# The last matmul stage of an attention and two-MoE kernel: operands of its Strassen products on VectorE alone, and a third output chunk ahead of the first product group

## The chip, the cores and the metric

The kernel runs on one core of one Trainium2 chip. The metric is device microseconds of one launch, from the first to the last instruction and what lies around it. Three runs of the kernel before took 625.68, 630.52 and 633.74 us; the median is 630.52.

## What is computed

Three parts run one behind the other. Attention with 12 heads mixes its scores over the heads before and after the softmax; its output, 896 tokens (two batches of 448) by 768, goes through two feed-forward layers:

```
x = attention(q, k, v, w_pre, w_post)       # (896, 768)
h = x @ w_in;   g = elu(h);   x = g @ w_out   # w_in (768, 2048), w_out (2048, 768)
h = x @ w2_in;  g = h * sigmoid(h);  out = g @ w2_out
```

The change lies in the last product, `g @ w2_out`. Everything is float32; each matmul operand is split in two parts, hi (the value rounded to the type that TensorE takes, fp32r) and lo (value minus hi), and a product is the sum hi*hi + hi*lo + lo*hi.

## The kernel before, in words

Output is held transposed: 6 row chunks c0 to c5 of 128 model columns, each by 896 tokens, that is by two halves of 448 tokens (each a matmul of 448 columns into one PSUM bank). The contraction over 2048 hidden units is 16 blocks f0 to f15 of 128. For f0 to f9 a chunk is computed classically, in two parts of five blocks (`moe_out`, line 527 and below): 5 blocks x 3 terms x 2 halves = 30 matmuls. The last six blocks f10 to f15 are done for two chunks at once by Strassen's scheme in Winograd's form: a 2x2 block product with seven products instead of eight. Each product (`prod2`, line 1050) is three blocks x three terms = 9 matmuls; seven make a pair of 63 matmuls. The left operands come from the weights, the right ones (B11, B21, B22, T1, T2, T3, T4) from the activations: B11 and T3's source are the first and second token half of f10 to f12, B21 and B22 those of f13 to f15; T1 = second half of f10 to f12 minus B11, T2 = B22 - T1, T3 = second half of f10 to f12 minus B22, T4 = B21 - T2. Each of the seven is split into hi (a cast on ScalarE) and lo (a subtraction on VectorE), for three blocks. They are made once, and all three pairs use them.

The program is written out by hand: each engine runs its instructions in the order of the code, and nothing is reordered. Engines are tied by semaphores. Around every chunk of weights stands the same row of work: a load of raw 64-bit words on SyncE's queue into one of two buffers (`load_w`, L435), a rescaling on ScalarE (`scale`, L755), two bit operations on VectorE (`bits0` and `bits1`, L746 and L751), a cast to hi on ScalarE (`split_hi`, L489), a subtraction to lo on VectorE (`split_lo`, L498). The result goes to one of four weight buffers (`wbuf`, tile `we`). A classical chunk takes one of the four, a Strassen pair all four (`hi_of` L735, `lo_of` L547, and sums of two weight chunks in `sums12`, `sum3`, `sum4`, L547 and L759). A chunk is loaded two chunks ahead, when the bit operations have emptied the raw buffer.

The order of the output stage (loop over j) is: classical parts of two chunks (120 matmuls), then their Strassen pair, three times. The first classical part of c0 lies already inside the end of the stage ahead, whose last products (lines 803 and 812 to 816) make f14 and f15; three classical parts (90 matmuls) then stand before the first pair. In these three parts `g_sums` (line 1024) makes the seven operands: one block at a time, 448 columns an instruction. The four subtractions T1 to T4 of each block, and the lo part of B22, go to GpSimd (POOL, L1030); the other lo parts go to VectorE (L547), the hi parts to ScalarE (L1034). In the pair, product B11 goes into a PSUM bank that ScalarE copies out (`one`, L1115) before product T2 adds to that bank.

Of the kernel before, what the change touches and what calls it, by code (L numbers as in the profile page):

```python
# [17 lines left out]
P = 128  # L18
# [17 lines left out]
KS = 10  # L36
KB = -(-S // BI)
# [38 lines left out]
def attn_moe_moe(ctx: ExitStack, tc: tile.TileContext, q, k, v, w_pre, w_post, w1i, w1o, w2i, w2o, out):  # L76
# [323 lines left out]
    for w in (w1i, w1o, w2i, w2o):  # L400
# [37 lines left out]
    def ring(n):  # L438
        return (O2 + (n - O2) % 6 if n >= O2 else n) % (NE + 1)
# [566 lines left out]
    x = [t[:, i] for t in rt for i in range(3)] + rk[:3]  # L1006
    for f in range(KF):
        raw[1, f] = x[f % 12]
    hb[1] = rk[3:]
    x = [ge[u][:, i] for u in range(2) for i in range(3)] + [gs[:, i] for i in range(6)]  # L1010
    x += [xt[1][a, i] for a in ("B11", "B21", "T2", "T1", "T3", "T4", "B22") for i in range(3)]
    for f in range(KS):
        gop[1, f] = x[2 * f:2 * f + 2]
    xs = x[2 * KS:]
    ob = [raw[1, f] for f in (4, 5)]
# [8 lines left out]
    def g_sums(i):  # L1024
        r1, r2 = raw[1, KS + i], raw[1, KS + 3 + i]
        t1, t2, t4 = (mo["eg"][:, j] for j in range(3))
        src = {"B11": r1[:, 0], "B21": r2[:, 0], "B22": r2[:, 1], "T1": t1, "T2": t2, "T3": r1[:, 1], "T4": t4}

        def psub(o, x, y):
            nc.gpsimd.tensor_tensor(o, x, y, op=ALU.subtract)  # L1030

        def sp(a):
            t = xt[2][a, i]
            nc.scalar.copy(t[:, 0], src[a])  # L1034
            (psub if a == "B22" else sub)(t[:, 1], src[a], t[:, 0])
# [12 lines left out]
    xs += [rg[:, i] for i in range(3)] + [None]  # L1048
    xt[2] = {(a, i): xs.pop(0) for a in ("T1", "T3", "B11", "B21", "T2", "B22", "T4") for i in range(3)}

    def prod2(o, d, u, x, start=False):
        hi, lo = wbuf[d]
        n_ = 0
        for wt, xi in ((hi, 0), (hi, 1), (lo, 0)):
            for i in range(3):
                nc.tensor.matmul(o, wt[:, u * KH + i * P:u * KH + (i + 1) * P], xt[2][x, i][:, xi], start=start and n_ == 0, stop=n_ == 8, skip_group_check=True)  # L1056
# [10 lines left out]
    def o_dma(c, hf, x=slice(0, S), eng=None):  # L1067
        (eng or nc.sync).dma_start(out[c * P:(c + 1) * P, hf * S + x.start:hf * S + x.stop], ob[hf][:, c % 2, x])

    def o_add(c, hf, a, parts=1):  # L1070
        for i in range(parts):
            x = slice(i * S // parts, (i + 1) * S // parts)
            nc.vector.tensor_tensor(ob[hf][:, c % 2, x], state[1, c][hf][:, x], a[:, x], op=ALU.add)
            o_dma(c, hf, x, (nc.sync, nc.scalar)[i])

    for j in range(3):
        n0, c0 = O2 + 6 * j, 2 * j
        a, b_ = n0 + 4, n0 + 5
# [122 lines left out]
```

## Time and profile before

| | |
|---|---|
| median of three runs | 630.52 us |
| profiled execution | 625.0 us, its span 623.2 us |
| mean granted TensorE clock | 0.989 of full |
| TensorE busy | 596.3 us, 96% of the span |
| VectorE busy | 457.7 us, 73% |
| ScalarE busy | 373.1 us, 60% |
| GpSimd busy | 84.9 us, 14% |

A busy TensorE is a modelled figure. The granted clock is the share of full speed that TensorE was given in a stretch: 1.0 is 2.4 GHz, 0.5 is 1.2 GHz. In the profile, PE is the matmuls, PEld the weight loads that overlap them, DVE is VectorE, ACT ScalarE, POOL GpSimd, SP SyncE; L1056 is line 1056 of the kernel before. Names of tiles stand without their numbers: `we` the weight buffers, `wr` raw weights, `wc` weights after the bit operations, `po` an output bank, `q` a Strassen bank, `rt` and `rk` activations, `eg` scratch.

### The profile page before, as it was taken

The numbers are of one execution on the slowest core, as the hardware profiler recorded it, in microseconds if no ns is written. First come the engines' busy times: TensorE is split into PE (matmuls) and PEld (weight loads), VectorE is DVE, ScalarE is ACT, GpSimd is POOL, SyncE is SP. The second block draws the span as 40 slices with busy tenths as digits, with TensorE's granted clock in tenths as the row PEclk, the third lists the DMA queues.
The fourth block names the chain that finished last, engine by engine and source line by source line (L and its number), as shares of the span: only waits on it lengthen the run. The fifth ranks groups of instructions, "written<-read, shape, count | busy, mean of one in ns | idle before, by whom it ended". The sixth has DMA issues, their size and how long they took to land.

```text
span 623.2 us, 15033 instructions
## 1 busy us (share of the span) xinstructions
PE 596.3 (96%) x6139; PEld 509.2 (82%) x6139; DVE 457.7 (73%) x761; ACT 373.1 (60%) x698; POOL 84.9 (14%) x132
## 2 busy tenths in 40 slices
PE   7899999998999999999999999999999997699997
PEld 3456666565799899999999999999999995599996
DVE  4776776787747998967775755798888889854552
ACT  4676776778748867578755533577766663532321
POOL 1222222257440000000000000000000326000000
PEclk9999999999999999999999999999999997799999
DMA  6587558745313343422334344243342231352701
GB/s 235 197 231 218 161 136 215 215 147 201 129 53 103 101 127 127 136 85 88 119 115 136 94 143 119 84 154 123 131 140 97 86 102 42 110 191 86 218 14 59
DMA packets 37682, 82.04 MB, mean 132 GB/s; under 512 B 4205, under 2 KB 18285, under 8 KB 37613
## 3 DMA queue, kind: packets, MB, share of 16 engines
q1 hardware_dynamic: 36749, 80.08, 41.0%
q8 instruction: 48, 0.79, 0.5%
q10 hardware_dynamic: 864, 1.00, 0.5%
q14 instruction: 21, 0.17, 0.1%
HBM read 59.05 MB, written 2.75 MB: 99 GB/s over the span
## 4 chain that ended last, share of the span: by engine, by line
PE 74%; DVE 11%; ACT 7%; DMA 4%; issue 2%; ACTq 0%; POOL 0%; DVEq 0%; SPq 0%; POOLq 0%
PE po L541 26%; PE b L803 25%; PE av L262 4%; ACT pe L209 4%; PE q L1056 3%; DMA blk<-s 3%; PE post L234 3%; PE pre L195 3%; PE ph L527 3%; PE pq L147 3%; PE po L1056 2%; DVE nmx L201 2%; DVE a L133 1%; PE post L527 1%; DVE rr L547 1%
## 5 line engine op out<-in xcount | busy, mean ns | idle before, releaser
L803 PE MATMUL b<-x,we 128*128 128x448 f32 x360 | 93.7, 363 | 0.0
L209 ACT ACTIVATE pe<-pre,nmx 124x448 f32<-124x448 f32 x90 | 56.3, 630 | 37.4 <-DVE nmx L201 36.5
L755 ACT ACTIVATE wr<-wr 128x768 f32<-128x768 f32 (+1 forms) x61 | 52.7, 864 | 36.7 <-DMA wr<-in_w2o_dram 21.9
L803 PEld LDWEIGHTS b<-x,we 128*128 128x128 f32 x360 | 67.5, 188 | 4.6
L803 PE MATMUL b<-rr,we 128*128 128x448 f32 x288 | 69.5, 362 | 0.0
L234 PEld LDWEIGHTS post<-krn,pe 60*64 60x64 f32 x2520 | 46.0, 135 | 22.7 <-issue 11.1
L541 PE MATMUL po<-gs,we 128*128 128x448 f32 x216 | 60.3, 362 | 0.0
L541 PE MATMUL po<-ge,we 128*128 128x448 f32 x216 | 60.3, 362 | 0.0
L751 DVE SCALAR_TENSOR_TENSOR wc<-wr,wc 128x768 int32<-128x768 int32 (+1 forms) x62 | 57.0, 920 | 2.7
L498 DVE TENSOR_TENSOR we<-wc,we 128x640 fp32r<-128x640 f32 (+1 forms) x31 | 27.7, 894 | 40.2 <-ACT we L489 40.1
L803 PEld LDWEIGHTS b<-rr,we 128*128 128x128 f32 x288 | 54.1, 188 | 3.5
L201 DVE TENSOR_REDUCE nmx<-pre 124x1 f32<-124x448 f32 x90 | 51.6, 614 | 5.2 <-PE pre L195 4.7
L541 PE MATMUL po<-x,we 128*128 128x448 f32 x204 | 54.4, 362 | 0.0
L222 POOL TENSOR_SCALAR krn<-kps,sum 124x60 f32<-124x60 f32 x90 | 37.8, 435 | 114.2 <-DVE sum L218 97.4
L234 PE MATMUL post<-krn,pe 60*64 60x60 f32 x2520 | 47.3, 219 | 4.1 <-POOL krn L222 2.8
L262 PEld LDWEIGHTS av<-a,v 128*64 128x64 f32 x768 | 36.9, 137 | 17.4 <-ACT pe L209 6.3
L195 PE MATMUL pre<-blk,kpre 64*64 64x448 f32 x360 | 47.4, 543 | 2.4 <-DMA blk<-s 1.7
L541 PE MATMUL po<-ta,we 128*128 128x448 f32 x168 | 44.8, 362 | 0.0
L147 PE MATMUL pq<-kt,qt 64*64 64x448 f32 x336 | 41.8, 564 | 2.8 <-ACT s L154 2.2
L1030 POOL TENSOR_TENSOR eg<-rk 128x448 f32<-128x448 f32 x2 | 2.9, 1436 | 300.9 <-ACT rk L816 300.9
L262 PE MATMUL av<-a,v 128*64 128x120 f32 (+1 forms) x768 | 41.8, 262 | 2.0 <-ACT a L131 2.0
L541 PEld LDWEIGHTS po<-ge,we 128*128 128x128 f32 x216 | 40.6, 188 | 2.6
(166 smaller groups left out, 1165.0 us busy)
## 6 DMA issues: line engine op xcount, KB each, us to landing
blk<-s SPq DMA_DIRECT2D x77, 210.0 KB
wr<-in_w1i_dram SPq DMA_DIRECT2D x32, 384.0 KB
wr<-in_w2i_dram SPq DMA_DIRECT2D x32, 384.0 KB
wr<-in_w1o_dram SPq DMA_DIRECT2D x24, 384.0 KB
wr<-in_w2o_dram SPq DMA_DIRECT2D x24, 384.0 KB
wr<-in_w1o_dram SPq DMA_DIRECT2D x12, 256.0 KB
wr<-in_w2o_dram SPq DMA_DIRECT2D x12, 256.0 KB
v<-in_v_dram SPq DMA_DIRECT2D x14, 192.0 KB
```

Source lines behind the costliest of these rows:

```text
L147: nc.tensor.matmul(pq[e][HS * c:HS * c + HS], qT[T][half, p, HS * c:HS * c + HS], kT[p][half, bs[c % len(bs)]], start=True, stop=True, til ...
L195: nc.tensor.matmul(pre[s][r][HS * c:HS * c + HS], kpre[o], blkb[o, s % NBUF, c], start=True, stop=True, tile_position=(HS * r, HS * c))
L201: nc.vector.tensor_reduce(nmx[s][:n, r:r + 1], pre[s][r][:n], axis=AX.X, op=ALU.max, negate=True)
L209: nc.scalar.activation(t[:n], pre[s][r][:n], AF.Exp, bias=nmx[s][:n, r:r + 1], scale=1.0, accum_out=sums[s][:n, r:r + 1])
L222: nc.gpsimd.tensor_scalar(t[:n], kps[:n], z[:n, r:r + 1], None, op0=ALU.mult)
L234: nc.tensor.matmul(w[c][HS * u:HS * u + HS, r, j * BW:(j + 1) * BW], pexp[s][r][o, m * HS:(m + 1) * HS], kr[s][r][o].rearrange("p h i -> p ...
L262: nc.tensor.matmul(avt[T][e * D:(e + 1) * D, p % 2, :m], vall[b][:NV, h, j], amap[T][:NV, j * H + h, :m], start=j == 0, stop=j == 3, tile_ ...
L541: nc.tensor.matmul(po, wt[:, kk * P:(kk + 1) * P], g_op(moe, k0 + kk, hf, gi), start=(k0 == 0 and n_ == 0), stop=(k0 + kn == (KF, KS)[moe] ...
L751: nc.vector.scalar_tensor_tensor(cc, r[:, :, 1], 3, cc, op0=ALU.logical_shift_left, op1=ALU.bitwise_or)
L755: nc.scalar.activation(hf, hf, AF.Prelu, scale=2.0 ** -112, alpha=2.0 ** 32)
L803: nc.tensor.matmul(o, wt[:, u * KH + i * P:u * KH + (i + 1) * P], X[x, i][:, xi], start=start and n_ == 0, stop=n_ == 8, skip_group_check= ...
L1056: nc.tensor.matmul(o, wt[:, u * KH + i * P:u * KH + (i + 1) * P], xt[2][x, i][:, xi], start=start and n_ == 0, stop=n_ == 8, skip_group_ch ...
```

## The change

It makes the operands for all three blocks at once: one instruction on three blocks x 448 columns, 1344 in all, for each hi, each lo and each of the subtractions T1 to T4, the subtractions on VectorE. Only B22's parts stay at 448 columns. GpSimd has no instruction left in this stage: its 15 subtractions go. For this the activations f10 to f15 and the operands get other homes (whole triples), and f0 to f9 move to make room. The chunks come in another order: both classical parts of c2 stand ahead of the first Strassen pair (c0, c1); c3's two parts stand between the first and the second pair (c2, c3); four parts of c4 and c5 stand between the second and the third. The operands are made in five steps (list `xtra`), one for each classical part, each behind the cast of the weights of the chunk after next. B11 and T1 are started in the end of the stage ahead. The result buffers are others. The number of matmuls is the same. All lines of the new kernel stand a little lower: L547 is L549, L1034 is L1043 or L1047, L1115 is L1093.

```
+OUT2 = ((0,), (1,), (2,), (0, 1), (3,), (2, 3), (4,), (5,), (4, 5))
...
-            for c in range(0, KC, 2):
-                for kb in ((0, 5), (5, 5), (KS, 6)):
-                    for e in range(2):
-                        chunks.append(("out", w, c + e, kb))
+            for x in OUT2:
+                for c in x if len(x) == 2 else x * 2:
+                    chunks.append(("out", w, c, (KS, 6) if len(x) == 2 else ((0, 5), (5, 5))[sum(y[2] == c and y[1] is w for y in chunks)]))
...
     def ring(n):
-        return (O2 + (n - O2) % 6 if n >= O2 else n) % (NE + 1)
+        if n >= O2:
+            n += 2 * sum(x[0] == "out" and x[3][0] == KS and i % 2 == 1 for i, x in enumerate(chunks[O2:n]))
+        return n % (NE + 1)
...
-    x = [t[:, i] for t in rt for i in range(3)] + rk[:3]
     for f in range(KF):
-        raw[1, f] = x[f % 12]
+        x = f + 2 if f < KS else f - KS
+        raw[1, f] = rt[x // 3][:, x % 3] if x < 9 else rk[x - 9]
     hb[1] = rk[3:]
     x = [ge[u][:, i] for u in range(2) for i in range(3)] + [gs[:, i] for i in range(6)]
-    x += [xt[1][a, i] for a in ("B11", "B21", "T2", "T1", "T3", "T4", "B22") for i in range(3)]
-    for f in range(KS):
+    x += [rr[u][:, i] for u in range(2) for i in range(3)]
+    for f in range(KS - 1):
         gop[1, f] = x[2 * f:2 * f + 2]
-    xs = x[2 * KS:]
-    ob = [raw[1, f] for f in (4, 5)]
...
-    def g_sums(i):
-        r1, r2 = raw[1, KS + i], raw[1, KS + 3 + i]
-        t1, t2, t4 = (mo["eg"][:, j] for j in range(3))
-        src = {"B11": r1[:, 0], "B21": r2[:, 0], "B22": r2[:, 1], "T1": t1, "T2": t2, "T3": r1[:, 1], "T4": t4}
-
-        def psub(o, x, y):
-            nc.gpsimd.tensor_tensor(o, x, y, op=ALU.subtract)
-
-        def sp(a):
-            t = xt[2][a, i]
-            nc.scalar.copy(t[:, 0], src[a])
-            (psub if a == "B22" else sub)(t[:, 1], src[a], t[:, 0])
-
-        psub(t1, r1[:, 1], r1[:, 0])
-        psub(t2, r2[:, 1], t1)
-        psub(r1[:, 1], r1[:, 1], r2[:, 1])
-        psub(t4, r2[:, 0], t2)
-        return [lambda a=a: sp(a) for a in ("B11", "B21", "T1", "T2", "T3", "T4", "B22")]
+    def gk(*ps):
+        return [kp.tile([P, 2, S], F32R, name=f"gk{p}", tag=f"kT{p}") for p in ps]
+
+    def last_homes():
+        gop[1, KS - 1] = gk(3, 5)
+
+    sx = {"B11": mo["x1"][:, :3], "B21": rr[2], "T2": rr[3], "T1": rr[4], "T3": mo["x1"][:, 3:]}
+    src = {"B11": rt[0][:, :, 0], "T1": rt[0][:, :, 0], "T3": rt[0][:, :, 1], "B21": rt[1][:, :, 0], "T4": rt[1][:, :, 0], "B22": rt[1][:, :, 1], "T2": mo["eg"][:, :3]}
+    dif = {"T1": ("T3", "B11"), "T2": ("B22", "T1"), "T3": ("T3", "B22"), "T4": ("B21", "T2")}
+
+    def gd(a):
+        return lambda: sub(src[a], *(src[x] for x in dif[a]))
+
+    def gx(a):
+
+        def go():
+            t = sx[a]
+            if a == "B22":
+                for i in range(3):
+                    nc.scalar.copy(t[i][:, 0], src[a][:, i])
+                for i in range(3):
+                    sub(t[i][:, 1], src[a][:, i], t[i][:, 0])
+            else:
+                nc.scalar.copy(t[:, :, 0], src[a])
+                sub(t[:, :, 1], src[a], t[:, :, 0])
+        return go
     e2[7, 6] = gsp(6, 7)
-    e2[8, 2] = gsp(8, 9)
+    e2[8, 2] = [last_homes] + gsp(8, 9)
+    e2[8, 4] = [gx("B11")]
+    e2[8, 5] = [gd("T1")]
     stage(1, I2, 0, 8, e2)
-    xs += [kp.tile([P, 2, S], F32R, name=f"gk{p}", tag=f"kT{p}") for p in (3, 4, 5, 0)]
-    rg = triple("t2", F32R, "rg")
-    xs += [rg[:, i] for i in range(3)] + [None]
-    xt[2] = {(a, i): xs.pop(0) for a in ("T1", "T3", "B11", "B21", "T2", "B22", "T4") for i in range(3)}
+    sx["T4"] = triple("t2", F32R, "rg")
+    sx["B22"] = gk(4, 1, 2)
+    xtra = [None, [gx("B21"), gd("T2"), gx("T2")], [gx("T1"), gd("T3")], [gx("T3"), gd("T4")], [gx("T4")], [gx("B22")]]
...
+    ob = {(0, 0): rk[0][:, 0], (1, 0): rk[0][:, 1], (1, 1): rt[0][:, 0, 0], (0, 1): rt[0][:, 0, 1]}
...
-    for j in range(3):
-        n0, c0 = O2 + 6 * j, 2 * j
-        a, b_ = n0 + 4, n0 + 5
-        d = [ring(n0 + i) for i in range(4)]
-        more = j < 2
-        for i in range(4):
-            n = n0 + i
-            if n == O2:
-                continue
-            if i == 3:
-                lo_of(d[0], fw(a))
-            elif n > O2 + 1:
-                split_lo(n + 1)
-            if j == 0 and i == 3:
-                xt[2]["T4", 2] = kp.tile([P, 2, S], F32R, name="gk1", tag="kT1")
-            tw_ = g_sums(i - 1) if j == 0 else []
-            for f in tw_[:3]:
-                f()
-            if i < 3:
-                conv(n + 2)
-            if i < 2:
-                split_hi(n + 2)
-            elif i == 2:
-                hi_of(d[0], fw(a))
-            else:
-                conv(b_)
-                sums12(a)
-                hi_of(d[1], s21)
-                sum3(a)
-                lo_of(d[1], s21)
-                sum4(a)
-                hi_of(d[2], fw(b_))
-            for f in tw_[3:]:
-                f()
-            moe_out(n, 1, *chunks[n][2:3], *chunks[n][3])
-        b1, b3 = (bank([P, S], f"q{k}_{j}") for k in "13")
+            nc.vector.tensor_tensor(y[:, x], state[1, c][hf][:, x], a[:, x], op=ALU.add)
+            (nc.sync, nc.scalar)[i].dma_start(out[c * P:(c + 1) * P, hf * S + x.start:hf * S + x.stop], y[:, x])
+
+    def strassen(n, c0):
+        d = [(ring(n) + i) % 4 for i in range(4)]
+        more = n + 2 < NCH
+        b1, b3 = (bank([P, S], f"q{k}_{n}") for k in "13")
...
+    n = O2 + 1
+    while n < NCH:
+        c, k = chunks[n][2:]
+        if k[0] == KS:
+            strassen(n, c)
+            n += 2
+            continue
+        i = n - O2
+        new = xtra[i] if i < len(xtra) else []
+        nx = [x[3][0] == KS for x in chunks[n + 1:n + 3]]
+        d = [(ring(n + 1) + i) % 4 for i in range(4)]
+        if nx[0]:
+            lo_of(d[0], fw(n + 1))
+        elif i > 1:
+            split_lo(n + 1)
+        conv(n + 2)
+        if nx[0]:
+            sums12(n + 1)
+            hi_of(d[1], s21)
+            sum3(n + 1)
+            lo_of(d[1], s21)
+            sum4(n + 1)
+            hi_of(d[2], fw(n + 2))
+        elif nx[1]:
+            hi_of(ring(n + 2), fw(n + 2))
+        else:
+            split_hi(n + 2)
+        for f in new:
+            f()
+        moe_out(n, 1, c, *k)
+        n += 1
```

VectorE, around the bit operations on the weights of c1's second part (`wc_6034`, in the change `wc_6028`), whose lo goes to buffer `we_2607`. Before:

```order
L547 TENSOR_TENSOR x_2883<-rk_5127,x_2883 128x448
L547 TENSOR_TENSOR x_2883<-rt_5123,x_2883 128x448
L547 TENSOR_TENSOR x_2883<-eg,x_2883 128x448
L746 TENSOR_SCALAR wc_6034<-wr_5927 128x640
L751 SCALAR_TENSOR_TENSOR wc_6034<-wr_5927,wc_6034 128x640
L547 TENSOR_TENSOR x_2883<-eg,x_2883 128x448
L547 TENSOR_TENSOR rr_4634<-rk_5127,rr_4634 128x448
L547 TENSOR_TENSOR rg<-eg,rg 128x448
L498 TENSOR_TENSOR we_2607<-wc_6034,we_2607 128x640
L547 TENSOR_TENSOR hr<-rk_5128,hr 128x448
```

And now the same stretch, up to the lo of c2's first part (`we_3019`):

```order
L549 TENSOR_TENSOR rt_5123<-rt_5123 128x3x448
L748 TENSOR_SCALAR wc_6028<-wr_5927 128x640
L753 SCALAR_TENSOR_TENSOR wc_6028<-wr_5927,wc_6028 128x640
L549 TENSOR_TENSOR rr_4635<-rt_5124,rr_4635 128x3x448
L549 TENSOR_TENSOR eg<-rt_5124,rt_5123 128x1344
L549 TENSOR_TENSOR rr_4636<-eg,rr_4636 128x3x448
L500 TENSOR_TENSOR we_2607<-wc_6028,we_2607 128x640
L748 TENSOR_SCALAR wc_6072<-wr_6013 128x640
L753 SCALAR_TENSOR_TENSOR wc_6072<-wr_6013,wc_6072 128x640
L549 TENSOR_TENSOR hr<-rt_5123,hr 128x3x448
L549 TENSOR_TENSOR rt_5123<-rt_5123,rt_5124 128x3x448
L500 TENSOR_TENSOR we_3019<-wc_6072,we_3019 128x640
```

Before, the split of the weights into `we_2607` stood behind six subtractions of 448 columns; now it stands behind four instructions of 1344 columns (`rt_5123` T1, then B21's lo, `eg` T2 and T2's lo), one of them ahead of the bit operations.

ScalarE, from the cast of the weights for the first pair to the copy of B11's product. Before:

```order
L735 CAST we_3494<-s_3468 128x768
L735 CAST we_2164<-wc_6151 128x768
L1034 CAST gk_6020<-eg 128x448
L1034 CAST hr<-rt_5123 128x448
L1034 CAST gk_6140<-eg 128x448
L1034 CAST rg<-rt_5124 128x448
L1115 COPY eg<-q_0_6203 128x448
```

Now:

```order
L737 CAST we_2607<-s_3468 128x768
L737 CAST we_3019<-wc_6201 128x768
L1043 CAST gk_6025<-rt_5124 128x448
L1043 CAST gk_6026<-rt_5124 128x448
L1043 CAST gk_6027<-rt_5124 128x448
L1093 COPY eg<-q_56_6251 128x448
L737 CAST we_3494<-s_3469 128x384
```

The copy out of the bank `q` stood behind four operand casts; it now stands behind the three casts of B22 (`gk`), which follow two casts of pair weights (`we_2607`, `we_3019`).

SyncE's queue issues the loads of c2's two parts (5 blocks each) where it issued those of the first pair (6 blocks each), and the latter after them; the first store of a result comes two loads later.

## Rows read from the trace of the kernel before

**Rows 1.** Busy time by stretch: PE, PEld, DVE, ACT, POOL, granted clock, DMA share, GB/s.
```profile
510.00:515.00 5.00, 5.00 (x27) 4.69 (x26) 5.00 (x5) 2.01 (x4) 4.92 (x4) 1.00 0.21 84
...
520.00:525.00 5.00, 1.72 (x5) 0.84 (x3) 5.00 (x6) 2.77 (x6) 3.48 (x3) 0.65 0.33 115
...
535.00:540.00 5.00, 4.45 (x15) 4.05 (x16) 4.58 (x6) 1.84 (x5) 1.39 (x1) 0.64 0.12 46
```

**Rows 2.** Chain of waits to the end: start us, us, engine, tile, line.
```profile
546.25 24.00 PE po L541 x120
...
615.85 1.81 PE po L1056 x9
...
619.98 0.30 DVE rt L1073
```

**Rows 3.** TensorE's waits, 515 to 545 us: total, times, longest.
```profile
PE q L1056 <- ACT eg L1115: 6.1, 1, 6.1
```

**Rows 4.** Timeline of TensorE: start us, us, line, operation, count, [idle before].
```profile
500.51 0.76 PE L541 MATMUL po<-ge,we 128*128 128x448 f32 x3
...
536.09 0.95 PE L1056 MATMUL q<-gk,we 128*128 128x448 f32 x2
...
538.33 0.70 PE L1056 MATMUL q<-gk,we 128*128 128x448 f32 x2
```

**Rows 5.** Groups by shape, 1344 columns: count, busy us, mean ns, idle before.
```profile
L547 DVE TENSOR_TENSOR ta<-xr,ta 128x1344 fp32r<-128x1344 f32 x3 | 4.7, 1558 | 2.2 <-ACT ta L656 2.2
...
L656 ACT CAST ta<-xr 128x1344 fp32r<-128x1344 f32 x3 | 4.0, 1321 | 0.0
```

**Rows 6.** Timeline of VectorE: start us, us, line, operation, tiles, shapes.
```profile
499.77 0.49 DVE L746 TENSOR_SCALAR wc<-wr 128x640 int32<-128x640 int32 x1
500.30 0.83 DVE L751 SCALAR_TENSOR_TENSOR wc<-wr,wc 128x640 int32<-128x640 int32 x1
501.04 0.62 DVE L812 TENSOR_TENSOR rk<-b,rk 128x448 f32<-128x448 f32 x1
502.92 0.83 DVE L498 TENSOR_TENSOR we<-wc,we 128x640 fp32r<-128x640 f32 x1 [1.26 <-ACT we L489]
...
511.65 1.57 DVE L547 TENSOR_TENSOR hr<-rk,hr 128x448 fp32r<-128x448 f32 x1
...
557.45 0.56 DVE L746 TENSOR_SCALAR wc<-wr 128x768 int32<-128x768 int32 x1
558.03 0.96 DVE L751 SCALAR_TENSOR_TENSOR wc<-wr,wc 128x768 int32<-128x768 int32 x1
...
562.41 0.56 DVE L759 TENSOR_TENSOR s<-wc 128x384 f32<-128x384 f32 x1
...
564.51 0.96 DVE L547 TENSOR_TENSOR we<-s,we 128x768 fp32r<-128x768 f32 x1 [0.48 <-ACT we L735]
```

**Rows 7.** Timeline of ScalarE.
```profile
498.37 0.53 ACT L816 ACTIVATE rt<-b 128x448 f32<-128x448 f32 x1
...
502.17 0.71 ACT L489 CAST we<-wc 128x640 fp32r<-128x640 f32 x1
502.79 0.79 ACT L755 ACTIVATE wr<-wr 128x640 f32<-128x640 f32 x1
...
508.21 0.56 ACT L1034 CAST rr<-rk 128x448 fp32r<-128x448 f32 x1
...
531.64 0.83 ACT L735 CAST we<-s 128x768 fp32r<-128x768 f32 x1 [5.83 <-DVE s L547]
```

**Rows 8.** Weight loads on SyncE's queue, and ScalarE's instructions that waited for them.
```profile
501.19 6.70 SPq L435 DMA_DIRECT2D wr<-in_w2o_dram  x4
...
506.09 0.93 ACT L755 ACTIVATE wr<-wr 128x768 f32<-128x768 f32 x1 [1.13 <-DMA wr<-in_w2o_dram]
...
549.10 4.37 SPq L435 DMA_DIRECT2D wr<-in_w2o_dram  x4
...
555.16 0.89 ACT L755 ACTIVATE wr<-wr 128x768 f32<-128x768 f32 x1 [5.32 <-DMA wr<-in_w2o_dram]
```

More of the change, by code (lines that the diff above doesn't have):

```diff
@@ L1051, in prod2 @@
     def prod2(o, d, u, x, start=False):
         hi, lo = wbuf[d]
+        t = sx[x]
         n_ = 0
@@ L1055, in prod2 @@
             for i in range(3):
-                nc.tensor.matmul(o, wt[:, u * KH + i * P:u * KH + (i + 1) * P], xt[2][x, i][:, xi], start=start and n_ == 0, stop=n_ == 8, skip_group_check=True)
+                nc.tensor.matmul(o, wt[:, u * KH + i * P:u * KH + (i + 1) * P], t[i][:, xi] if x == "B22" else t[:, i, xi], start=start and n_ == 0, stop=n_ == 8, skip_group_check=True)
                 n_ += 1
@@ L1065, in conv @@
             scale(n + 1)
-    def o_dma(c, hf, x=slice(0, S), eng=None):
-        (eng or nc.sync).dma_start(out[c * P:(c + 1) * P, hf * S + x.start:hf * S + x.stop], ob[hf][:, c % 2, x])
+    ob = {(0, 0): rk[0][:, 0], (1, 0): rk[0][:, 1], (1, 1): rt[0][:, 0, 0], (0, 1): rt[0][:, 0, 1]}
     def o_add(c, hf, a, parts=1):
+        y = ob[c % 2, hf]
         for i in range(parts):
             x = slice(i * S // parts, (i + 1) * S // parts)
-            nc.vector.tensor_tensor(ob[hf][:, c % 2, x], state[1, c][hf][:, x], a[:, x], op=ALU.add)
-            o_dma(c, hf, x, (nc.sync, nc.scalar)[i])
-    for j in range(3):
-        n0, c0 = O2 + 6 * j, 2 * j
-        a, b_ = n0 + 4, n0 + 5
-        d = [ring(n0 + i) for i in range(4)]
-        more = j < 2
-        for i in range(4):
-            n = n0 + i
-            if n == O2:
-                continue
-            if i == 3:
-                lo_of(d[0], fw(a))
-            elif n > O2 + 1:
-                split_lo(n + 1)
-            if j == 0 and i == 3:
-                xt[2]["T4", 2] = kp.tile([P, 2, S], F32R, name="gk1", tag="kT1")
-            tw_ = g_sums(i - 1) if j == 0 else []
-            for f in tw_[:3]:
-                f()
-            if i < 3:
-                conv(n + 2)
-            if i < 2:
-                split_hi(n + 2)
-            elif i == 2:
-                hi_of(d[0], fw(a))
-            else:
-                conv(b_)
-                sums12(a)
-                hi_of(d[1], s21)
-                sum3(a)
-                lo_of(d[1], s21)
-                sum4(a)
-                hi_of(d[2], fw(b_))
-            for f in tw_[3:]:
-                f()
-            moe_out(n, 1, *chunks[n][2:3], *chunks[n][3])
-        b1, b3 = (bank([P, S], f"q{k}_{j}") for k in "13")
+            nc.vector.tensor_tensor(y[:, x], state[1, c][hf][:, x], a[:, x], op=ALU.add)
[4 more added lines that the diff above has]
+        b1, b3 = (bank([P, S], f"q{k}_{n}") for k in "13")
         one, z, y = (mo["eg"][:, k] for k in range(3))
         prod2(b1, d[0], 0, "B11", True)
-        lo_of(d[2], fw(b_))
+        lo_of(d[2], fw(n + 1))
         nc.scalar.copy(one, b1)
@@ L1122, in attn_moe_moe @@
         if more:
-            conv(n0 + 6)
+            conv(n + 2)
         prod2(b3, d[1], 1, "T1", True)
         if more:
-            split_hi(n0 + 6)
-            split_lo(n0 + 6)
+            split_hi(n + 2)
+            split_lo(n + 2)
         nc.vector.tensor_tensor(z, b3, z, op=ALU.add)
@@ L1131, in attn_moe_moe @@
         if more:
-            conv(n0 + 7)
-            split_hi(n0 + 7)
+            conv(n + 3)
+            split_hi(n + 3)
         prod2(state[1, c0 + 1][0], d[2], 1, "T4")
@@ L1139, in attn_moe_moe @@
         o_add(c0, 1, z, 1 if more else 2)
+    n = O2 + 1
[13 more added lines that the diff above has]
+            split_lo(n + 1)
+        conv(n + 2)
+        if nx[0]:
[8 more added lines that the diff above has]
+        else:
+            split_hi(n + 2)
+        for f in new:
+            f()
+        moe_out(n, 1, c, *k)
+        n += 1
     cm_m.__exit__(None, None, None)
```

## The prediction

> **What bounds the kernel now.** I began with the stretches of the output stage [rows 1]. From 510 to 515 us TensorE is busy throughout at full clock; from 520 to 525 us it is busy for 1.72 us of 5, and the granted clock averages 0.65 (part of the stretch at 1.2 GHz). The reader is to see who works instead: VectorE, 5.00 of 5 us, and GpSimd. The chain of waits says what this costs. Outside this gap matmuls are all that counts: 120 take 24.00 us, 0.2 us each [rows 2]. The last classical stretch ahead of the first pair starts at 500.51 [rows 4] and has 90 matmuls, so the pair could start at 518.5. From there 429 matmuls are left (three pairs of 63, eight parts of 30), 85.8 us, which would end at 604.3. In the trace T4 of the last pair starts at 615.85 [rows 2] and B22 follows it, 18 matmuls, to 619.45. **15.1 us are lost**, all before 546.25, where the chain has its first unbroken 120 matmuls. The waits name the largest piece: 6.1 us for ScalarE's copy of B11's product [rows 3], which stands in ScalarE's order behind operand casts. The operands come too late. The rest is smaller waits for operands and matmuls at 0.373 us (six in the 2.24 us from 536.09 to 538.33 [rows 4]), 1.2 GHz.
>
> **What goes and what comes.** GpSimd's 15 subtractions go. They cost more than their own time: VectorE's 448-column subtraction takes 1.57 us beside them (the row at 511.65), against 0.62 for a 448-column operation by itself (at 501.04) [rows 6]. VectorE gets ten instructions of 1344 columns, priced by the same shape in an earlier stage: 1.56 us on VectorE, 1.32 us for ScalarE's cast [rows 5]. Ten of them, 15.6 us, and three of 0.62 replace 18 of 448 columns. c2's two parts give 12.0 us of matmuls to hide them in. Moving c2 also moves its loads ahead of the first pair's on SyncE's queue; they are smaller (640 columns for 768). c0's second part is moved ahead of c1's first by 6 us; its last operand, f9's lo, stands in VectorE's order ahead of the bit operations of 499.77 [rows 6] and is needed ten matmuls into the part, at 502.3, so I cost that at nothing. The cover is some 2 us; past it every microsecond counts. Store order and homes: nothing, no one waits for them in the stretch.
>
> **The new order, step by step.** It decides, since both engines work in order. I add durations from the rows. A dependent instruction starts 0.04 us after the end of what it waits for (ScalarE's cast ends at 502.88 [rows 7], VectorE starts at 502.92 [rows 6]); an independent one starts 0.09 us ahead of the end of the one before it (501.13 and 501.04 [rows 6]).
>
> *Start.* B11's hi follows the Silu of 498.37 [rows 7] and ends at 500.1. VectorE, free at 501.04, does B11's lo to 502.60, the last addition of the stage ahead to 503.13; then ScalarE's last Silu (0.58) and cast (0.72), VectorE's weight lo (0.82) to 505.22, T1 to 506.70, and the bit operations for c1's second part (1.36, first two rows of [rows 6]) to 507.97.
>
> *c1's second part.* ScalarE casts its weights and then B21 (0.04 + 0.63 + 1.30 + 0.04); VectorE starts B21's lo at 509.98, T2 at 511.45, ends T2 at 513.01; ScalarE casts T2; T2's lo runs from 514.39 to 515.95. Only then comes the weights' lo, to 516.68. TensorE starts this part at 512.5 and needs the lo after ten matmuls, at 514.5: **a wait of 2.2 us**, end of the part 520.7.
>
> *c2's first part.* Bit operations to 517.95, cast of weights and T1, then T1's lo, T3 and the weights' lo to 523.72. TensorE needs it at 522.7: **1.0 us**, end 527.8. *Its second part:* the same row of work takes 7.05 us against 6.0 of matmuls; lo at 530.77, needed at 529.8: **1.0 us**, end 534.8.
>
> *The pair.* Bit operations for 768 columns (1.55, the rows at 557.45 and 558.03 [rows 6]) to 532.2; cast (0.83 [rows 7]) and T4's cast, T4's lo to 535.9, the pair's first lo (0.96) to 536.8. TensorE needs it after six matmuls, at 536.0: **0.8 us**; B11 and B21 end at 539.2. Bit operations to 538.2, two sums of 384 columns (0.56 each) to 539.4, casts of the sum and of the next weights (0.83), three casts of B22 (0.56 [rows 7], 0.47 apart), and only then the copy of B11's product, which ends at 542.9. T2 waits for it: **3.7 us**.
>
> So 8.8 us of the 15.1 stay. T2 starts at 542.94, 45 matmuls of the pair end at 551.9, then 306 (c3, the pair, four parts, the pair) in 61.2 us: 613.1 in place of 619.45, **6.3 us less**. With c3 alone between pairs one and two, the weights of pair two must be ready within 12.0 us of classical matmuls. Per part VectorE has at most a lo of 0.96, bits of 1.55, four sums of 0.56 and another lo, with their overlaps 5.4 us of 6.0. I cost that at nothing; the cover is some 3 us.
>
> *The clock.* The trace has no wait of 3.7 us by itself. In the first pair matmuls still took 0.373 us behind the wait of 6.1 us [rows 3, 4], at 1.2 GHz; a product, nine matmuls at 0.173 us more, loses 1.6 us so. Bounds: nothing if the clock stays, 3.1 if two products run like that behind the last wait. I take 1.6, the nearer to the row: from 520 to 525 us, where TensorE had shorter waits than the 3.7 us here, the granted clock averaged 0.65 [rows 1]. Falls in the smaller waits ahead cost nothing: the next waits, 6.5 us in all, absorb them.
>
> One rule speaks against the overlap of 0.09 us. The Trainium skill, VectorE: DVE Perf Modes, section "The DRAIN you can't avoid", says that the next VectorE operation does not start before the pipe is empty (it refers to another section for ones that start earlier). The rows at 501.04 speak against it here; by that rule fourteen overlaps on this path would go, 1.3 us, and the forecast would be 627.1.
>
> **Sum.** 625.0 (profiled execution) - 6.3 + 1.6 = 620.3. That execution lies 5.5 us below the median of the three runs, 630.5; the same 4.7 us off the median give **625.8 us**. Durations that are off by a tenth in the ten instructions move the end by about 1 us, so this case alone reaches from 623.2 to 628.4.
>
> **Rivals.**
> 1. *All is recovered* (0.15): VectorE and ScalarE get ahead of TensorE and every wait goes, 15.1 us, 615.4 (2.4% faster). For it: without GpSimd VectorE gains about 0.95 us on each operation that lay beside it, and two parts more hide the work. Against it: the ping-pong between the two engines, 9.98 us for the first step and 7.05 for the next two against 6.0. It decides at c1's second part: if the weights' lo is there by 514.5, this rival is on.
> 2. *Half clock through the waits* (0.06), slower than before: after the 2.2 us wait in c1's second part TensorE stays at 1.2 GHz until the pair's T2. 98 matmuls from 516.7 at 0.373 end at 553.3, 10.4 us behind 542.9; the kernel takes 634.6, 4.1 us more than before. It decides once more than 74 of them are that slow: 6.5 us of waits to absorb and 6.3 us of gain, at 0.173 us a matmul. For it: the fall in the trace came with waits no longer than that. Against it: the clock came back as soon as TensorE had worked without a break, and a slower TensorE has no waits.
> 3. *Loads late* (0.07): ScalarE's rescaling stands in its order ahead of casts, and each load starts only after the bit operations that empty its buffer. I have 4.9 us from issue to rescaling (501.19 to 506.09) and 6.1 at most (549.10 to 555.16) [rows 8]. From 6.2 on each microsecond more delays three steps, 3 us; at 9 us the first pair is 8.1 us later: 633.9. Against it: the loads moved up are the smaller ones, and no stores run then.
>
> **Chances and range.** Forecast 0.72, rivals 0.15, 0.06, 0.07. A measurement of this kernel can tell about 2%, 12.6 us, from no change. Only rival 1 passes that, and not surely: faster 0.14; rivals 2 and 3 stay within it: slower 0.03, for what I don't see; same 0.83. The range takes in the forecast's own case, the spread of the median (the runs differ by 8 us) and part of rivals 1 and 3: 617 to 631.5.
>
> **What would show it.** GpSimd without an instruction from 480 us on; ten VectorE instructions of 1344 columns near 1.56 us, none at 1.57 us for 448. TensorE's waits: about 2 us for the weights' lo in c1's second part, twice 1 us in c2, under 1 us in the pair's B11, 3 to 4 us for the copy of B11's product, nothing later. The clock at 1.2 GHz once behind the last wait. I am wrong if TensorE has no wait in c1's second part, if the last wait is not ScalarE's copy, if a later pair waits, or if the clock stays down for more than a few microseconds behind T2.

## The result, and the profile after

The changed kernel takes **619.89 us** (median of six runs, 617.45 to 622.17), where the kernel before took 629.19 (median of six, the three known ones among them): a ratio of 0.9852, 95% interval 0.9804 to 0.9899. That is 9.3 us less; 4.7 less were forecast, and 625.8 us. A second sample (c_after, below) gives 0.9901 (0.9868 to 0.9933), 6.2 us less by the ratio. Both are a gain, and both lie within 2%. The profiled execution took 619.49 us, its span 617.7, 5.5 us less than the 623.2 of before. TensorE is busy for 97%, VectorE for 73% (450.9 us), GpSimd for 62.9 us in place of 84.9; it has no instruction from 480 us on.

Stretches of the output stage, columns as in [rows 1]:

```profile
510.00:515.00 5.00, 4.55 (x23) 3.94 (x22) 3.53 (x4) 2.07 (x4) 0.00 (x0) 1.00 0.05 10
520.00:525.00 5.00, 5.00 (x27) 4.69 (x26) 2.93 (x3) 1.95 (x2) 0.00 (x0) 1.00 0.53 156
535.00:540.00 5.00, 1.55 (x5) 1.16 (x4) 4.52 (x9) 3.80 (x7) 0.00 (x0) 0.74 0.41 131
540.00:545.00 5.00, 5.00 (x16) 4.44 (x15) 2.92 (x6) 1.83 (x3) 0.00 (x0) 0.58 0.42 100
```

The gap that lay at 520 us is gone; a shorter one stands at 535, and the clock falls behind it (0.58 at 540 us, and sixteen matmuls in 5 us where 27 are normal, as in the first row of [rows 1]). What TensorE waited for from 500 us on (total, times, longest) answers to [rows 3]:

```profile
PE q L1066 <- ACT eg L1093: 3.5, 1, 3.5
PE po L543 <- DVE we L500: 2.1, 3, 0.8
PE q L1066 <- DVE we L549: 0.4, 1, 0.4
```

These are the five waits that were forecast, each for the thing forecast: ScalarE's copy of B11's product (last), the weights' lo in c1's second part and c2's two parts, and the pair's first lo. Their places, in the timeline of TensorE (start, duration, [idle before], as in [rows 4]):

```profile
497.81 0.36 PE L543 MATMUL po<-gs,we 128*128 128x448 f32 x1
...
512.41 0.47 PE L543 MATMUL po<-gs,we 128*128 128x448 f32 x1 [0.45 <-DVE we L500]
...
519.46 0.87 PE L543 MATMUL po<-ge,we 128*128 128x448 f32 x3 [0.78 <-DVE we L500]
...
526.55 0.47 PE L543 MATMUL po<-gs,we 128*128 128x448 f32 x1 [0.82 <-DVE we L500]
526.86 0.78 PE L543 MATMUL po<-rr,we 128*128 128x448 f32 x3
...
532.62 0.88 PE L1066 MATMUL q<-x,we 128*128 128x448 f32 x3 [0.44 <-DVE we L549]
533.33 1.96 PE L1066 MATMUL po<-rr,we 128*128 128x448 f32 x9
538.75 3.73 PE L1066 MATMUL q<-rr,we 128*128 128x448 f32 x9 [3.45 <-ACT eg L1093]
542.27 2.90 PE L1066 MATMUL q<-hr,we 128*128 128x448 f32 x9
545.01 2.02 PE L1066 MATMUL q<-x,we 128*128 128x448 f32 x9
```

Reckoned at 0.2 us a matmul from the first row, 70 matmuls on, the second start was due at 511.81: TensorE is 0.6 us late there, then by 0.9, 1.0, 0.6 and 3.6 us at the next four, each reckoned from the second matmul behind the wait ahead of it at the pitch in force there, 6.7 us in all (8.8 forecast). Nine matmuls behind the last wait take 3.52 us, until 542.27: 0.39 each. From 526.86 on there is something that the trace of before doesn't have: in the x3 rows three matmuls take 0.78 us and not 0.76, because they follow one another by 0.2067 us and not by 0.2. That shows in the end of the chain of waits too, which answers to [rows 2]:

```profile
538.75 8.29 PE q L1066 x27
547.04 3.72 PE po L1066 x18
550.76 12.40 PE po L543 x60
...
576.18 24.80 PE po L543 x120
```

120 matmuls take 24.80 us; before they took 24.00 [rows 2]. From 547.04 no wait is left in the chain's matmuls.

### The profile page after: what moved, and what is told of

Same layout as the page of the kernel before. It is cut to its first block, busy times and chain, and to the rows that moved or that the text cites. A ratio compares the mean times of both kernels' runs of the same rounds, so it can differ in the third digit from the quotient of the medians.

```text
span 617.7 us, 14991 instructions
## 1 busy us (share of the span) xinstructions
PE 596.6 (97%) x6139; PEld 507.6 (82%) x6139; DVE 450.9 (73%) x756; ACT 371.6 (60%) x686; POOL 62.9 (10%) x117
## 4 chain that ended last, share of the span: by engine, by line
PE 74%; DVE 10%; ACT 9%; issue 3%; DMA 3%; ACTq 0%; POOL 0%; DVEq 0%; POOLq 0%
PE b L805 27%; PE po L543 25%; ACT pe L210 4%; PE av L263 4%; PE q L1066 4%; PE ph L529 3%; PE post L235 3%; PE pre L196 3%; PE pq L148 3%; PE po L1066 2%; DMA blk<-s 2%; DVE nmx L202 2%; DVE a L134 2%; PE post L529 1%; DMA kt<-in_k_dram 1%
## 5 line engine op out<-in xcount | busy, mean ns | idle before, releaser
L543 PE MATMUL po<-x,we 128*128 128x448 f32 x192 | 50.1, 362 | 0.0
L543 PEld LDWEIGHTS po<-gs,we 128*128 128x128 f32 x216 | 40.5, 187 | 5.1 <-DVE we L500 2.0
```

The source lines that it names most:

```text
L543: nc.tensor.matmul(po, wt[:, kk * P:(kk + 1) * P], g_op(moe, k0 + kk, hf, gi), start=(k0 == 0 and n_ == 0), stop=(k0 + kn == (KF, KS)[moe] ...
```

## The experiments

Four theories stood against one another. **A** (the prediction's): the order of work between VectorE and ScalarE sets the waits, and c2's 12 us of matmuls are the cover; the other edits matter little. **B**: the gain is VectorE's time, freed from GpSimd beside it. **C**: the wide instructions are what is worth something. **D**: the waits come from VectorE's total work, not from its order. The expectations use these letters. To compare profiles I take the time from the first classical matmul behind the stage ahead (500.51 before, 497.81 after) to the end of the last matmul, that one counted at 0.2 us ("the stage"): 118.8 us before, 116.0 after; 519 matmuls at 0.2 are 103.8.

**c_before** and **c_after** are the two kernels again, in twelve runs each, the first against itself.

> The kernel before once more, unchanged. Both theories: ratio 1.00 to itself within half a per cent. What it is for: the stage behind the last mixing step of the attention part starts its weights' bit operations at 181.5 us in the profile of before and at 178.8 us in that of the changed kernel, in code that the change does not touch. If that is scatter from run to run, this profile has it elsewhere by 1 to 3 us; if the change moved it, it stands at 181.5 again.

> The changed kernel once more, unchanged. Theory A (the order of work on VectorE and ScalarE sets TensorE's waits): the same five waits again, 0.5, 0.8, 0.8, 0.4 and 3.5 us, ratio 0.985. Second question: behind the waits matmuls came every 0.2067 us, ahead of them every 0.2. If that belongs to the new order it is there again in all 300 matmuls, 2 us; if it is chance, it may be 0.2.

Measured: 0.9982 (0.9948 to 1.0015) and 0.9901 (0.9868 to 0.9933); 0.985 had been expected for the second, and lies outside its interval, though the two samples' intervals overlap. The spans are 623.0 and 619.1 us, the stage 118.9 and 112.9. c_after has the waits of the first profile (3.4; 2.0 in three; 0.4). Less was lost to the clock, and its matmuls are back at 0.2 us from 549 us on. Its stage is 3.1 us shorter than in the first profile of the change, and yet its span is 1.4 us longer; that comes from elsewhere. The same bit operation late in the attention part, which the change doesn't touch, in the first profile and in c_after:

```profile
178.80 0.56 DVE L479 SCALAR_TENSOR_TENSOR wc<-wr,wc 128x384 int32<-128x384 int32 x1 [1.26 <-ACT wr L457]
```

```profile
183.31 0.56 DVE L479 SCALAR_TENSOR_TENSOR wc<-wr,wc 128x384 int32<-128x384 int32 x1 [1.26 <-ACT wr L457]
```

From there to the first classical matmul it is 319.0 us in both (497.81 and 502.29), and in every other profile of this study. So the attention part scatters by some microseconds from run to run (178.8 to 185.3 in eleven profiles; in the two latest the granted clock had fallen on the way there, to a mean of 0.66 from 106 to 111 us in e_lo and of 0.57 from 8 to 12 and from 49 to 53 us in e_both), and of the 5.5 us between the first two spans 2.7 are that scatter, and 2.8 the stage. c_before alone would not have told: it stands at 181.15, close to the 181.5 of the first profile of before. c_after does, 4.5 us from the first profile of the same kernel.

**e_ops**: the new operands, the old order of the chunks.

```
-OUT2 = ((0,), (1,), (2,), (0, 1), (3,), ...
+OUT2 = ((0,), (1,), (0, 1), (2,), (3,), ...
-    xtra = [..., [gx("T3"), gd("T4")], [gx("T4")], [gx("B22")]]
+    xtra = [..., [gx("T3"), gd("T4"), gx("T4"), gx("B22")]]
```

> New operands (VectorE alone, 1344 columns), old order: only c0 and c1 ahead of the first pair, T4 and B22 made in c1's second part. Theory A: two weight chunks less to convert but 12.0 us less to hide in; by the durations of the rows the pair waits 2.3 us in B11 and 9 us for the copy of B11's product, 11.8 us in all against 7.0 with c2 ahead, and the clock falls for longer: 625 to 628 us. Theory B (what was won is VectorE's time lost beside GpSimd): no worse than the changed kernel, 619 to 622 us.

Measured: 0.9988 (0.9953 to 1.0023), no change. TensorE's waits:

```profile
PE q L1066 <- ACT eg L1093: 9.0, 1, 9.0
PE q L1066 <- DVE we L549: 1.9, 1, 1.9
PE po L543 <- DVE we L500: 0.5, 1, 0.5
```

The operands alone, in this form, give nothing, though GpSimd is idle here too. The stage takes 118.5 us, and the copy of B11's product is now 9.0 us late, where it was 6.1 [rows 3]: the wide casts of T3 and T4 and the three of B22 stand ahead of it in ScalarE's order, and the one of T4 waits for VectorE's subtraction. B falls as the cause of the gain; the sum of durations in program order (9 and 2.3 forecast, 9.0 and 1.9 measured) holds. What the same operands would do in the old order in pieces of 448 columns was not run.

**e_pool**: the new order, but T1 to T4 on GpSimd again, three blocks of 448 columns each.

```
     def gd(a):
-        return lambda: sub(src[a], *(src[x] for x in dif[a]))
+        def go():
+            for i in range(3):
+                x, y = (src[b][:, i] for b in dif[a])
+                nc.gpsimd.tensor_tensor(src[a][:, i], x, y, op=ALU.subtract)
+        return go
```

> New order, T1 to T4 by GpSimd again (three instructions of 448 columns each), the rest of VectorE's work as in the change. Theory A: T2 takes 4.5 us in place of 1.56 in the chain of c1's second part, 3 us, and VectorE's instructions beside GpSimd take about 0.95 us more each, against four of 1.47 us that it is spared; the first pair 2 to 5 us later, 622 to 625 us. Theory B: all of it is lost, 627 to 630 us.

Measured: 0.9868 (0.9826 to 0.991), not to be told from c_after. A had expected it slower than the change, and missed. GpSimd's subtractions, and VectorE beside them:

```profile
500.47 3.96 POOL L1038 TENSOR_TENSOR rt<-rt 128x448 f32<-128x448 f32 x3 [319.12 <-DVE x L549]
504.38 4.22 POOL L1038 TENSOR_TENSOR eg<-rt,rt 128x448 f32<-128x448 f32 x3
```

```profile
508.54 1.56 DVE L549 TENSOR_TENSOR rr<-rt,rr 128x1344 fp32r<-128x1344 f32 x1 [2.07 <-ACT rr L1051]
510.02 2.52 DVE L549 TENSOR_TENSOR rr<-eg,rr 128x1344 fp32r<-128x1344 f32 x1
```

GpSimd is slow, 4.2 us for T2, but it is a third engine: T2 is ready at 508.60, when ScalarE comes to cast it (508.63), and T2 no longer stands between two steps of the ping-pong. VectorE is rid of four instructions, 1.47 us each with their overlap, 5.9 us. Beside GpSimd seven others pay between 0.3 and 0.96 us (2.52 in place of 1.56 in the row at 510.02), 5.7 us in sum. The two sums come out even. Moving the subtractions to VectorE, the first thing that I had named under what goes, is worth nothing here; with e_ops, it is the order of the chunks that carries the gain.

**e_448**: the changed kernel with VectorE's ten wide instructions and ScalarE's casts ahead of them cut into three of 448 columns each (T1 to T4 likewise, not shown).

```
-                nc.scalar.copy(t[:, :, 0], src[a])
-                sub(t[:, :, 1], src[a], t[:, :, 0])
+                for i in range(3):
+                    nc.scalar.copy(t[:, i, 0], src[a][:, i])
+                for i in range(3):
+                    sub(t[:, i, 1], src[a][:, i], t[:, i, 0])
```

> The change with its ten instructions of 1344 columns cut back into three of 448 each, still on VectorE and ScalarE, in the new order. Theory A (the handing to and fro between the two engines in program order): ScalarE's first 448-column cast is done after 0.56 us in place of 1.31, so VectorE starts 0.75 us earlier in each of four steps, against some 0.13 us more for three instructions than for one; TensorE's waits ahead of the last fall from 2.5 us to about 1, the last (3.4 us) stays: 1 to 2 us less than the changed kernel. Rival C (the wide instructions are what the change is worth, since each instruction has a fixed cost): 2 to 4 us more than the changed kernel.

Measured: 0.9829 (0.9771 to 0.9887), 619.8 against 628.49 us. The profiled execution is the fastest of the six (612.99 us; its granted clock 0.999, the others' 0.992 to 0.997), so its stage of 108.0 us flatters this kernel. One wait is left:

```profile
PE q L1071 <- ACT eg L1098: 3.5, 1, 3.5
```

```profile
506.49 1.70 DVE L549 TENSOR_TENSOR rr<-rt,rr 128x448 fp32r<-128x448 f32 x3 [1.32 <-ACT rr L1051]
508.10 1.69 DVE L549 TENSOR_TENSOR eg<-rt,rt 128x448 f32<-128x448 f32 x3
```

Three pieces take 1.69 us where one wide instruction takes 1.55. But VectorE starts when ScalarE's first piece is cast: it idles 1.32 us ahead of B21's lo, not 2.08 (the row at 505.60 below), and not at all ahead of T2's lo. The four weight waits go. C falls: width costs, since it makes each step of the ping-pong wait for a whole triple. The timed gain over the change is not settled, the intervals overlap; that the four waits would go altogether was more than expected (about 1 us of them was to stay).

**e_lo**: in the changed kernel, the weights' lo directly behind their hi, ahead of the operands.

```
-        if nx[0]:
+        if nx[0] and i > 5:
             lo_of(d[0], fw(n + 1))
-        elif i > 1:
+        elif nx[0]:
+            pass
+        elif i > 5:
             split_lo(n + 1)
...
             split_hi(n + 2)
+            if i < 5:
+                split_lo(n + 2)
```

> The change with one thing moved: VectorE's lo part of the weights of c1's second part and of c2's two parts, and the pair's first lo, each directly behind ScalarE's cast of the same weights and ahead of the wide operand instructions. VectorE sat idle 2 us there in each step. Theory A: the four waits for the weights' lo (0.45, 0.75, 0.80, 0.44 us) go, the last wait stays at 3 to 4 us with its fall of the clock: 2 to 3 us less than the changed kernel. Rival D (the waits are not made by the order but by what VectorE has to do in all): the waits stay, no change.

Measured: 0.9833 (0.9785 to 0.988), 618.5 us, by the times not to be told from the first sample of the change; one wait left:

```profile
PE q L1066 <- ACT eg L1093: 4.1, 1, 4.1
```

The same instructions in another order, and four of five waits are gone: D falls. The last wait takes part of it back, 4.1 us for 3.5, since TensorE now arrives earlier. The profiled execution is the slowest of the six (622.34 us), and its stage is no shorter than c_after's, 113.0 us: 103.8, the wait of 4.1, 2.8 lost to the clock behind it and 2.2 to the pitch of 0.2067, which stays to the end here.

**e_both**: e_lo, and B22's casts and lo behind the second copy out of the bank, so that the copy of B11's product no longer stands behind them.

```
-    xtra = [..., [gx("T4")], [gx("B22")]]
+    xtra = [..., [gx("T4")]]
...
         nc.scalar.copy(z, b1)
+        if c0 == 0:
+            gx("B22")()
```

> As the kernel with the early lo, and B22's casts and lo behind the second copy out of the first pair's bank, so that the copy of B11's product doesn't stand behind them. Theory A: the last wait falls from some 3.9 to 2.5 us; whether the clock still falls behind it is open: 4 us less than the changed kernel if it does, 6 if it doesn't. Rival D: no change against the changed kernel.

Measured: 0.9784 (0.9732 to 0.9835), 616.92 us, the stage 108.9. The last wait is 2.7 us, in place of 4.1, and the clock still fell behind it. What is left of it: the copy still stands behind two weight casts, and these begin only when VectorE's second sum is done. A wait of 0.3 us for an output bank is new.

**e_best**: e_both, and T4's hi and lo and one rescaling of weights behind the copy of B11's product as well.

```
-    xtra = [..., [gx("T3"), gd("T4")], [gx("T4")]]
+    xtra = [..., [gx("T3"), gd("T4")]]
...
         lo_of(d[3], s4)
+        if more:
+            scale(n + 2)
+        if c0 == 0:
+            gx("T4")()
```

> As the kernel before it, and T4's cast and lo and the rescaling of the raw weights after next also behind the copy of B11's product. Nothing is then ahead of that copy but the pair's own weights. Theory A: no wait above 1 us, no fall of the clock, 8 us less than the changed kernel, about 15 less than the kernel before (0.976). Rival D: no change against the changed kernel. A rival in between: with T4 and B22 made inside the pair, a later product waits for them, up to 2 us.

Measured: 0.9761 (0.9716 to 0.9806), **614.11 us** (612.81 to 616.04): faster than both kernels; its interval lies clear of c_after's and just touches that of the first sample of the change. The stage is 106.6 us, 2.8 over the 103.8 of bare matmuls, and five of its six executions have a mean granted clock of 1.000, where the eighteen of the changed kernel have 0.992 to 0.999. Its waits, and the instructions that cause the new one:

```profile
PE po L543 <- DVE rt L1083: 1.4, 1, 1.4
PE q L1066 <- ACT eg L1093: 0.9, 1, 0.9
```

```profile
538.10 1.56 DVE L549 TENSOR_TENSOR rg<-rt,rg 128x1344 fp32r<-128x1344 f32 x1 [1.21 <-ACT rg L1047]
539.58 1.69 DVE L549 TENSOR_TENSOR gk<-rt,gk 128x448 fp32r<-128x448 f32 x3
...
547.76 1.16 DVE L1083 TENSOR_TENSOR rt<-po,eg 128x448 f32<-128x448 f32 x2
```

The lo parts of T4 and B22 now lie in the pair, so the additions that empty the pair's banks come late on VectorE, and the next classical part waits for a bank: 1.4 us, where no wait above 1 had been expected.

**Ahead of T2, with little of clock and pitch in it.** The clock fell behind the last wait in some profiles and not in others, so stages and times mix two things. What the order makes can be read ahead of that: the time from the first classical matmul to the start of T2 in the first pair, less 0.2 us for each matmul between (108 in the old order, 168 in the new).

| | start to T2, us | lost, us |
|---|---|---|
| before, c_before | 35.04, 35.06 | 13.4, 13.5 |
| after, c_after | 40.94, 40.94 | 7.3, 7.3 |
| e_ops | 33.83 | 12.2 |
| e_pool | 39.35 | 5.8 |
| e_448 | 37.67 | 4.1 |
| e_lo | 37.88 | 4.3 |
| e_both | 36.49 | 2.9 |
| e_best | 34.66 | 1.1 |

Each kernel that was profiled twice repeats to 0.02 us. The change gains 6.1 us here, the operands alone 1.2, and with the subtractions on GpSimd in the new order (e_pool) 1.6 us less is lost than in the change. In e_pool VectorE's two sums came out even, but T2 is out of the ping-pong, and one weight wait of 1.1 us stands where the change has three, 2.1 in all. The pieces of 448 columns (e_448) and the early lo (e_lo) lose 3.3 and 3.1 us less than the change, by one profile each.

**e_gp**: the changed kernel with four more GpSimd subtractions of 448 columns where the kernel before ran its first four, 18 us ahead of the stage; no one reads their result.

```
+    du = mo["eg"][:, 3]
+    def busy():
+        for _ in range(4):
+            nc.gpsimd.tensor_tensor(du, rt[1][:, 0, 1], rt[0][:, 0, 0], op=ALU.subtract)
+    e2[7, 2] = [busy]
```

> The changed kernel with four extra GpSimd subtractions of 448 columns in the place where the kernel before ran its first four (behind the Silu of f13's second half, some 18 us ahead of the output stage). Their result is read by no one. What it tells apart: why the first wait was 0.6 us where 2.2 were forecast. If it is VectorE's lead from the absence of GpSimd there: the four VectorE instructions beside them (bits, lo of two weight chunks) take 1.3, 1.6, 1.9 and 1.8 us as before in place of 0.5, 0.8, 1.0 and 0.8; the last bit operation ahead of the stage ends about 0.6 us behind TensorE's first classical matmul (in the changed kernel 1.27 us ahead of it), c1's second part starts behind a wait near 2.2 to 2.5 us instead of 0.5, the other waits stay at 0.8, 0.8, 0.4 and 3.5, and from the first classical matmul to the end it takes about 1.9 us more than the 112.9 to 116.0 of the two profiles of the changed kernel, as far as clock and pitch behind the waits agree. If the lead comes from elsewhere (the other order of the operands f0 to f9, their homes): the first wait stays at 0.5.

Measured, in one execution: span 618.6 us. GpSimd works from 483.63 to 489.68, and VectorE's instructions in that time, then the same two of the change without it (first profile after):

```profile
485.24 1.60 DVE L753 SCALAR_TENSOR_TENSOR wc<-wr,wc 128x640 int32<-128x640 int32 x1
486.76 1.91 DVE L549 TENSOR_TENSOR we<-wc,we 128x768 fp32r<-128x768 f32 x1
...
501.37 0.82 DVE L753 SCALAR_TENSOR_TENSOR wc<-wr,wc 128x640 int32<-128x640 int32 x1
```

```profile
480.60 0.83 DVE L753 SCALAR_TENSOR_TENSOR wc<-wr,wc 128x640 int32<-128x640 int32 x1
481.53 0.96 DVE L549 TENSOR_TENSOR we<-wc,we 128x768 fp32r<-128x768 f32 x1
...
495.71 0.83 DVE L753 SCALAR_TENSOR_TENSOR wc<-wr,wc 128x640 int32<-128x640 int32 x1
```

```profile
517.99 0.47 PE L543 MATMUL po<-gs,we 128*128 128x448 f32 x1 [1.77 <-DVE we L500]
```

The last bit operation ahead of the stage ends at 502.19, 0.1 us behind the first classical matmul (502.06); in the change it ends 1.3 us ahead of it (496.54 and 497.81). The first wait, 0.45 us in the change, is 1.77 with GpSimd busy; the others stay at 0.8, 0.8, 0.4 and 3.4. The expectation had 0.6 us behind and a wait of 2.2 to 2.5: the mechanism is there, with 1.3 us more of wait where 1.7 to 2.0 more were expected; VectorE came in 0.1 us behind, and not 0.6. The stage took 112.6 us, no longer than in c_after, since the clock stayed at 1.00 behind the last wait here.

## Why the prediction was right, and where it was off

**The order sets the waits: right.** Against [rows 6], VectorE after:

```profile
505.60 1.56 DVE L549 TENSOR_TENSOR rr<-rt,rr 128x1344 fp32r<-128x1344 f32 x1 [2.08 <-ACT rr L1047]
507.07 1.55 DVE L549 TENSOR_TENSOR eg<-rt,rt 128x1344 f32<-128x1344 f32 x1
510.06 1.56 DVE L549 TENSOR_TENSOR rr<-eg,rr 128x1344 fp32r<-128x1344 f32 x1 [1.44 <-ACT rr L1047]
511.54 0.82 DVE L500 TENSOR_TENSOR we<-wc,we 128x640 fp32r<-128x640 f32 x1
```

The wide instructions take 1.55 and 1.56 us, as priced from [rows 5], and they stand in the order in which I added them. From the start of one chunk's bit operations to the next the steps take 10.17, 7.04 and 7.09 us; 9.98, 7.05 and 7.05 were forecast. An independent instruction still starts 0.09 us ahead of the end of the one before (505.60 + 1.56 = 507.16; the next starts at 507.07), so the 1.3 us that the forecast weighed against this overlap were not lost. The last wait is where it was put; VectorE's second sum and ScalarE after, against [rows 7]:

```profile
534.65 0.56 DVE L549 TENSOR_TENSOR s<-s,wc 128x384 f32<-128x384 f32 x1
```

```profile
535.30 0.83 ACT L737 CAST we<-s 128x768 fp32r<-128x768 f32 x1 [2.51 <-PE po L1066]
536.04 0.83 ACT L737 CAST we<-wc 128x768 fp32r<-128x768 f32 x1
536.77 1.49 ACT L1043 CAST gk<-rt 128x448 fp32r<-128x448 f32 x3
538.17 0.52 ACT L1093 COPY eg<-q 128x448 f32<-128x448 f32 x1
```

Two weight casts and B22's three, and only then the copy, for which T2 waits 3.5 us (3.7 forecast). The first row puts ScalarE's idle 2.51 us down to TensorE, whose product B21 ends at 535.29 by the profile. But the cast reads that sum of VectorE's, which ends at 535.21, 0.09 us ahead of it; in c_after, with the same 0.09 us, the wait is put down to the sum. So the last wait too hangs on VectorE's order, two steps back. e_both and e_best, which take B22 and T4 out from ahead of the copy, have waits of 2.7 and 0.9 (e_lo, from which they start, 4.1).

**The first wait: mis-sized.** The step "Start" took VectorE's place at 501.04 from the trace of before, half a microsecond behind the first classical matmul, and forecast 2.2 us. But GpSimd's first subtractions had slowed VectorE on its way there, and those I had counted only from 510 us on; with them gone it arrives 1.3 us ahead. TensorE is 0.6 us late in place of 2.2, and that is most of the difference between 6.7 and 8.8. e_gp brings the wait back to 1.77 with the rest unchanged, so this cause is shown for 1.3 of the 1.6 us; the rest is open.

**The clock: the right middle, no constant.** I took 1.6 us, between 0 and 3.1. Behind the same last wait the loss is 2.7 us in the first profile (18 matmuls from 538.75 to 545.01, 6.26 us for 3.6), 1.7 in c_after, and none in the profiles of e_448 and e_gp. From 540 to 545 us, just behind the wait of 3.5 us that ends at 536.95, the row of e_448 has all 27 matmuls at full clock:

```profile
540.00:545.00 5.00, 5.00 (x27) 4.69 (x26) 3.60 (x6) 1.55 (x3) 0.00 (x0) 1.00 0.64 203
```

**What was not foreseen: the pitch of 0.2067 us,** some 2.4 us in the first profile. The stage then adds up: 103.8 + 6.7 of waits + 0.1 for each of four restarts + 2.7 + 2.4 = 116.0. The forecast had 103.8 + 8.8 + 1.6 = 114.2; the two profiles have 116.0 and 112.9, on either side. That the first profiled execution (619.5 us) comes so near the 620.3 of the forecast's sum is luck: its stage is 1.8 us longer than forecast, and its attention part was 2.7 us shorter.

**The sum.** Against the stage of before, 4.7 us less were forecast; the profiles give 2.8 and 6.0, the runs 9.3 (6.4 to 12.3 by the interval) and 6.2 (4.2 to 8.3). The direction and the mechanism hold, and the real gain is probably somewhat larger than forecast. Ahead of T2 both profiles gain 6.1 us, where 13.4 - 8.8 = 4.6 were forecast; behind it the change lost 5.1 us to clock and pitch in the one and 1.7 in the other, where the kernel before lost 1.7. What the rest of the 9.3 consists of is not shown: the attention part alone moves by up to 6.5 us between runs.

**The rivals.** *All recovered* needed the weights' lo of c1's second part 14.0 us behind the first classical matmul; it came after 14.55 (512.36), and the three waits behind it came as well. *Half clock through the waits*: the granted clock is 1.00 from 510 to 515 and from 520 to 525, and it fell at the last wait alone (0.74 and 0.58). *Loads late*: no wait on the path ends with ScalarE's rescaling. And what I costed at nothing (c0's second part moved ahead, the loads, pair two with c3 alone as cover) shows no wait in the trace.

**The reason given for GpSimd: true, but not the source of the gain.** I wrote that its subtractions cost more than their own time, as a thing that the change gets rid of. They do slow VectorE, and in the trace of before that lies on the path to the copy: of VectorE's instructions from 509.95 to 529.4 us ten take 0.9 to 1.0 us longer than by themselves, two of them here, and the sum that the cast at 531.64 [rows 7] waited for comes behind them.

```profile
521.61 1.90 DVE L547 TENSOR_TENSOR we<-wc,we 128x768 fp32r<-128x768 f32 x1
523.43 1.54 DVE L547 TENSOR_TENSOR x<-rt,x 128x448 fp32r<-128x448 f32 x1
```

But e_ops (no GpSimd, no gain) and e_pool (GpSimd, full gain) show that taking the subtractions over on VectorE, in wide instructions, costs about what it frees.

## What to carry to other kernels

When two engines hand work back and forth in program order, count what stands ahead of the one instruction that the bottleneck waits for. Reordering the chunks gave the gain here (e_ops to c_after), and a few lines more gave about as much again in e_best; moving the subtractions from GpSimd to VectorE gave nothing. And an anchor taken from the old trace must be cleaned of what the change removes ahead of it, not only in the place where the change is made.

## What the runs showed of the hardware that I had not expected

- VectorE pays mostly 0.8 to 0.95 us on an instruction beside a GpSimd subtraction, whatever its width among these: 0.83 to 1.60 and 0.96 to 1.91 us at 640 and 768 columns (e_gp), 1.56 to 2.52 at 1344 (e_pool). In proportion the narrower of them suffer most.
- Behind a wait of 3.4 to 3.5 us TensorE's granted clock fell to 0.5 in some profiles (first profile, c_after, e_pool) and not in others (e_448, e_gp); behind 2.7 us it fell in e_both. The length of the wait doesn't tell them apart. What does is open.
- The pitch of matmuls went from 0.2 to 0.2067 us behind a wait in five of eleven profiles, with the granted clock at 1.00, and went back behind a later one or not at all (first profile, e_lo). No run tells why.
